# Retention into a maxout FFN: first weight loads moved ahead of a value load, the first two products cut into column parts, conversion steps put before copies

## The chip, the cores and the metric

The kernel runs on one core of a Trainium2 chip. The metric is device time in microseconds (us), measured around one execution; the profile's span runs from the first to the last instruction that the profiler recorded. All times below are us unless ns is written.

## The reference

Inputs: q, k, v of shape (8 batches, 8 heads, 576 positions, 64) in float32, and weights w1, w2, w3 (512 x 768) and w_out (768 x 512) in float64. What must come out:

```
scores = q k^T / sqrt(64)
D[i, j] = gamma_h ** (i - j)  for i >= j, else 0
attn    = (scores * D) v                       # per batch and head
x       = attn, put together to 4608 x 512     # token rows, heads side by side
h       = max(x w1, x w2, x w3)
out     = h w_out                              # 4608 x 512
```

## The kernel before, in words

The 4608 tokens are 36 **chunks** of C = 128 rows (a name with g is a chunk) and 9 **blocks** of 512 tokens, four chunks each (t is a block). A chunk's retention is a causal product within the chunk plus a carried state of 64 x 64 per head. For the first chunks the steps are functions called by hand, in the order in which their instructions go into the engines' queues:

- `load(g)` (L225): three transfers of 256 KB (k, q, v) on SP's queue; a chunk that crosses a batch's end has two halves each. The fourth chunk (CPT - 1 = 3) puts the load of one weight piece before its v, at L230.
- `transposes(g)` (L254): TensorE (PE) transposes k and q into PSUM, ScalarE (ACT) copies them out as kT and qT (L272).
- `scores(g)` (L274): 8 matmuls of qT and kT (L285), then VectorE (DVE) multiplies the two results by the causal mask into `st` (L201 is the recorded line of such steps).
- `decay(g)` (L241): GpSimd (POOL) scales v into `vd` (L249). `state(g)`: 8 matmuls `kv` (L352). `keep(g)`: DVE, and where a state goes on POOL too, makes the next state (L360 to L363).
- `values([g])` (L375): 8 matmuls of vd and st (L393), 8 of state and qT (L406), then `output` (L441): two DVE multiplications by `gq` into this chunk's columns of xT.

PE takes its queue in order, so a matmul that waits holds all that follow it. The same holds for DVE, ACT, POOL and SP.

Weights come as 24 **pieces** of 512 KB (18 of w1 to w3, each 128 columns wide, then 6 of w_out), each in two transfers of 256 KB (`load_weights`, L485). They are 64-bit floats, and `convert_all` (L614) turns them into fp32. Per pair of pieces there are the steps exponent (DVE L630, ACT L632), fraction (ACT L638, DVE L639, ACT L641), whole (DVE L644), sign (DVE L648) and product (DVE L656, which writes `w`); the first three pairs go piece by piece, and from the fifth on the exponent of the next pair is put before the sign and product of the one at hand (L692). `convert(n)` runs the next n steps of this list. Each finished piece asks for one more load. Six pieces are asked for at the start, and there is room for eight.

A transfer uses one of eight semaphores in turn (ACT's and SP's together), and an issue waits until the transfer eight places earlier has landed.

Block 0 is the stretch in which everything is still being loaded and converted. In `ffn(0)` (L791) nine units (fp, i) follow each other, each with two plain products `up_plain` (L779) of 128 x 512 outputs over a depth of 512, then `downs_plain`. The first product of all was already split: 384 columns, which need chunks 0 to 2, and 128 columns, which need chunk 3. After each product comes its `maximum`: an ACT copy (i = 0, L789) or a DVE maximum (L788). Between the units the steps for block 1's chunks 4 to 7 are woven in (`steps(1)`, L911): `scores(4)`, `state(4)` and `keep(4)` come right after the first unit. From block 1 on the work is a sparser product scheme (L760, L557) on converted weights.

The order before the first unit is written out from L867 on: loads of chunks 0 to 3 with the two small `gs` transfers on SP after chunk 1, one weight piece, chunk 4, four pieces; then chunk by chunk the steps above, all of chunk 3 done before the first product starts; `gq` is loaded by four ACT issues after the first transposes.

Of the kernel before, what the change touches and what calls it, by code (L numbers as in the profile page):

```python
# [45 lines left out]
ALU = mybir.AluOpType  # L46
PSUM = bass.MemoryType.PSUM

C = 128
NT = 4 * C  # L50
# [31 lines left out]
def kernel(  # L82
# [14 lines left out]
    nc = tc.nc  # L97
    P = 128
    B, H, S, D = q.shape
# [25 lines left out]

    gk = const.tile([C, H], FP32, name="gk")
    gs_of = const.tile([P, H], FP32, name="gs_of")
    gs = const.tile([P, NP], FP32, name="gs")  # L130
# [1 line left out]
    const.tile([P, FILL // 4], FP32, name="fill")  # L132
    gq = const.tile([P, NP, C], FP32, name="gq")
    nc.scalar.dma_start(gk[:], key_decay)
    nc.vector.memset(one[:], 1.0)
    nc.scalar.copy(first[:], one[:])

# [11 lines left out]
    def warm(n):  # L149

        ps = ps_y.tile([P, P], FP32, tag="y", name="warm")
        for _ in range(n):
            nc.tensor.matmul(ps[:], lhsT=ident[:], rhs=ident[:], start=True, stop=True)
# [15 lines left out]
    def spans(g):  # L169

        row = 0
        while row < C:
# [1 line left out]
            n = min(C - row, S - pos)  # L174
            yield row, b, pos, n
            row += n

    def half(j):
        return slice(D * j, D * (j + 1))

    def place(g, c):

# [39 lines left out]
                        t[r:r + 32, :, e, :],  # L222
                        src[b, :, pos:pos + 32, 32 * a:32 * a + 32].rearrange("h p i -> p h i"))

    def load(g):  # L225
        if g >= BY_PE and ("q", g) not in raws:
            load_blocks(g, *range(C // 32))
        for n, src in (("k", k), ("q", q), ("v", v)) if g < BY_PE else (("k", k), ("v", v)):
            if n == "v" and g == CPT - 1:
                load_weights(1)  # L230
            bufs = {"k": 3, "q": 2, "v": 4}[n]
            pool, bufs = (raw0, 1) if n != "v" and g < BY_PE and g % (bufs + 1) == bufs else (raw, bufs)
            if n == "v":
                t = vpool.tile([C, H, D], FP32, tag="v", name="vraw")
            else:
                t = pool.tile([C, H, D], FP32, tag=n, name=n + "raw", bufs=bufs)
            raws[n, g] = t
            for row, b, pos, m in spans(g):
                nc.sync.dma_start(t[row:row + m], src[b, :, pos:pos + m, :].rearrange("h p d -> p h d"))

    def decay(g):  # L241
        factor = gk[:].unsqueeze(2).to_broadcast([C, H, D])
# [6 lines left out]
        nc.gpsimd.tensor_tensor(vds[g][:], t[:], factor, op=ALU.mult)  # L249
# [479 lines left out]
    def convert(n):  # L729
        for _ in range(n):  # L730
            next(converting, None)
# [44 lines left out]
                    nc.sync.dma_start(out[t * NT + m * P:t * NT + (m + 1) * P, :], osb[:])  # L776
            yield

    def up_plain(t, h, fb, i):  # L779
        ps = (ps_x, ps_y)[fb % 2].tile([P, NT], FP32, tag="xy"[fb % 2], name="up")  # L780
        first_of_all = t == 0 and (fb, i) == (0, 0)
        for cols in (slice(0, NT - C), slice(NT - C, NT)) if first_of_all else (slice(0, NT),):
            for dc in range(NDC):
                nc.tensor.matmul(ps[:, cols], lhsT=w_sb[i, fb][:, dc * P:(dc + 1) * P], rhs=xT[t][:, dc, cols],  # L784
                                 start=dc == 0 and cols.start == 0, stop=dc == NDC - 1,
                                 skip_group_check=first_of_all)
        if i > 0:
            return lambda: nc.vector.tensor_tensor(h[:, fb, :], h[:, fb, :], ps[:], op=ALU.max)  # L788
        return lambda: nc.scalar.copy(h[:, fb, :], ps[:])  # L789

    def ffn(t):  # L791

        h = hpool.tile([P, NF, NT], FP32, tag="h", name="h")
        if t == 0:
            for fp, i in units:
                for fb in (2 * fp, 2 * fp + 1):
                    maximum = up_plain(t, h, fb, i)
                    if CPT not in qks:
                        maximum()
                        transposes(CPT)  # L800
                        convert(4)
                        continue
                    if (fp, i) == units[-1]:
                        maximum()
                        convert(2)
                        continue
                    convert(4 if (fp, i) in units[:2] else 2)
                    maximum()
                yield
            convert(3)  # L810
            for fb, _ in enumerate(downs_plain(t, h)):
                convert(2 if fb < 2 else 4 * len(pieces))
                if fb == 2:
                    while_converting.close()
                    late["pool"] = ctx.enter_context(tc.tile_pool(name="late", bufs=1))
                    late_room()
                    sums_of_outs()
                elif fb > 2:
                    chore({3: 4, 4: 0, 5: 2}[fb])
                if fb in (1, 3):  # L820
                    yield
            yield
            return
        if t == 1:
            spread.append(True)
            weight_sums(0)
            weight_sums(2)
        plain = 1 if t == 1 else None
        order = (1, 0, 2) if t == 1 else (0, 2, 1)
        total = sum(48 if fp == plain else 2 * len(PRODUCTS) for fp in order)  # L830
        count = parts = 0
        for fp in order:
            if fp != plain:
                while fp not in summed_fp:
                    chore()
            for step, cost in enumerate(up_plain_all(t, h, fp) if fp == plain else up(t, h, fp)):
                if fp == plain:
                    chore(4 if step == 4 else 8)
                elif step % 4 == 1 or step % 4 == 3 and len(urgent) > (2 if t == 1 else 6):
                    chore(len(urgent) > 0)  # L840
                elif step % 4 == 2 and chores and (t > 1 or NF // 2 - 1 not in summed_fp):
                    chores.popleft()()
                if step % 3 == 2:
                    scale()
                count += cost or 1
                if count * (NF // 2 * 3) >= (parts + 1) * total:
                    parts += 1
                    yield
            sums_of_hidden(h, fp)
            if fp == plain:  # L850
                weight_sums(fp)
        chore(len(urgent))
        for n, _ in enumerate(downs(t, h, order)):
            chore(4)
            scale(2)
            if n in (1, 3):
                yield
        yield

    def up_plain_all(t, h, fp):  # L860
        for fb in (2 * fp, 2 * fp + 1):
            for i in range(3):
                up_plain(t, h, fb, i)()
                yield 8


    warm(6)  # L867
    for g in range(CPT):
        load(g)
        if g == 1:  # L870
            for j in range(2):
                nc.sync.dma_start(gs[half(j)].unsqueeze(2), state_decay[half(j), :, D * j:D * j + 1])
    load_weights(1)
    load(CPT)
    load_weights(4)
    decay(0)
    transposes(0)
    for c in range(2):
        for b in range(2):
            nc.scalar.dma_start(gq[half(c), b::2, :], out_decay[half(b), NP // 2 * c:NP // 2 * (c + 1), :])  # L880
    warm(2)
    scores(0)
    transposes(1)
# [4 lines left out]
    scores(1)  # L888
    first_output()
    transposes(2)  # L890
    state_factors()
    decay(2)
    state(1)
    keep(1)
    values([1], [1])
    transposes(3)
    decay(3)
    scores(2)
    scores(3)
    state(2)  # L900
    keep(2)
    convert(2)
    values([2], [2])
    convert(2)
    values([3], [3])
    convert(4)
    keep(3)
    decay(CPT)
    convert(2)

    def steps(t):  # L911

# [97 lines left out]
```

## Time and profile before

| | us |
|---|---|
| median of 4 runs | 755.0 |
| lowest and highest of them | 754.3, 756.08 |
| profiled execution's own time | 754.3 |
| its span | 752.2 |
| PE busy | 744.3 (99% of the span) |
| DVE, ACT, POOL busy | 510.0, 319.8, 82.6 |
| granted TensorE clock | 1.000 |
| start of the first product of block 0 (PE L784) | 25.17 |
| start of the second unit of block 0 | 34.85 |
| start of block 0's down products (PE L771) | 99.76 |

PE is busy nearly all the time, so the page's averages say little about the change. Read the order of time instead: the timelines of the engines over the first 100 us, in which a bracket says how long the engine stood idle before a row and what ended that, and the list of what PE waited for. A row of a timeline gives start, length, engine, line, operation, output and inputs, and the count of instructions merged; PE rows count two passes for each matmul. A row's length includes the tail of its last instruction, so the next row of the same engine may start before it ends.

### The profile page before, as it was taken

The page shows a single profiled execution, that of the slowest core. Times are in us where ns is not written, and L with a number is a line of the kernel's source. Part 1 is how long each engine was busy: PE and PEld are TensorE (multiplying, and loading weights), DVE is VectorE, ACT ScalarE, POOL GpSimd, SP SyncE. Part 2 cuts the span into 40 slices and gives each one's busy share as a digit, 9 for nine tenths or more (in the row PEclk, how much of TensorE's full clock was granted, in tenths as well). Part 3 has the DMA queues.
Part 4 walks back from the last instruction along what each step waited for, and adds up shares of the span by engine and source line. Part 5 has one row for each costly group of instructions (what it writes and reads, how often), then busy time and mean ns, then how long its engine had stood idle before and what let it go on. Part 6 is the DMA issues. An engine that isn't in the chain of part 4 may idle for free.

```text
span 752.2 us, 16566 instructions
## 1 busy us (share of the span) xinstructions
PE 744.3 (99%) x6728; PEld 607.8 (81%) x6728; DVE 510.0 (68%) x856; ACT 319.8 (43%) x645; POOL 82.6 (11%) x103
## 2 busy tenths in 40 slices
PE   8899999999999999999999999999999999999998
PEld 7545545588888888888888888888888888888887
DVE  3998987857866765686567746675667656763662
ACT  3674531055245433544354335542454245414441
POOL 3110112002000100011010101010101010100000
PEclk9999999999999999999999999999999999999999
DMA  9996742505142514242343224232515141000001
GB/s 222 225 245 142 223 93 72 98 16 99 44 94 40 93 37 101 50 78 50 75 83 66 63 65 91 40 75 66 95 29 95 44 93 36 1 30 29 0 1 57
DMA packets 230204, 59.30 MB, mean 79 GB/s; under 512 B 210800, under 2 KB 228848, under 8 KB 230128
## 3 DMA queue, kind: packets, MB, share of 16 engines
q1 hardware_dynamic: 229264, 57.91, 35.6%
q8 instruction: 53, 0.87, 0.5%
q10 hardware_dynamic: 864, 0.33, 0.2%
q14 instruction: 23, 0.19, 0.1%
HBM read 48.76 MB, written 9.44 MB: 77 GB/s over the span
## 4 chain that ended last, share of the span: by engine, by line
PE 94%; DVE 3%; DMA 2%; SPq 1%; issue 0%; ACT 0%; ACTq 0%; DVEq 0%
PE a L760 19%; PE b L760 16%; PE dx L557 11%; PE up L784 8%; PE c L760 8%; PE dz L557 6%; PE e L760 5%; PE d L760 5%; PE sk L307 3%; PE down L771 3%; PE dy L557 3%; PE o L424 2%; PE o L431 2%; DMA bits<-in_moe_w_out_dram 1%; PE kv L310 1%; PE o L393 1%
## 5 line engine op out<-in xcount | busy, mean ns | idle before, releaser
L748 DVE TENSOR_TENSOR part<-part 128x512 f32<-128x512 f32 x161 | 111.3, 691 | 107.5 <-ACT part L745 105.2
L745 ACT COPY part<-b 128x512 f32<-128x512 f32 x115 | 67.4, 586 | 154.8 <-PE b L760 154.8
L748 DVE TENSOR_TENSOR h<-h,part 128x512 f32<-128x512 f32 x115 | 79.5, 691 | 29.1 <-ACT h L745 25.1
L784 PE MATMUL up<-xT,w 128*128 128x512 f32 (+2 forms) x200 | 85.0, 579 | 1.5 <-DVE w L656 1.5
L745 ACT COPY part<-a 128x512 f32<-128x512 f32 x92 | 53.9, 586 | 49.5 <-PE a L760 49.0
L784 PEld LDWEIGHTS up<-xT,w 128*128 128x128 f32 x200 | 36.7, 190 | 43.9 <-issue 39.9
L760 PE MATMUL a<-s,w 128*128 128x256 f32 x276 | 70.9, 379 | 0.0
L760 PE MATMUL b<-s,n 128*128 128x256 f32 x276 | 70.8, 379 | 0.0
L189 ACT ACTIVATE vraw<-vraw,gk 128x64 f32<-128x64 f32 x208 | 65.5, 347 | 1.0 <-DMA vraw<-in_v_dram 1.0
L760 PEld LDWEIGHTS b<-s,n 128*128 128x128 f32 x276 | 52.4, 190 | 7.1
L760 PEld LDWEIGHTS a<-s,w 128*128 128x128 f32 x276 | 52.4, 190 | 7.1
L527 POOL TENSOR_TENSOR H<-h 128x256 f32<-128x256 f32 x24 | 20.3, 844 | 310.1 <-DVE h L748 310.1
L760 PE MATMUL c<-xT,w 128*128 128x256 f32 x184 | 49.1, 389 | 0.0
L760 PE MATMUL b<-xT,n 128*128 128x256 f32 x184 | 47.2, 379 | 0.0
L760 PE MATMUL d<-s,w 128*128 128x256 f32 x184 | 47.2, 379 | 0.0
L324 POOL TENSOR_TENSOR s<-s,gs_of 64x512 f32<-64x512 f32 x21 | 22.5, 1070 | 211.1 <-DVE s L322 209.1
L557 PE MATMUL dx<-To,H 128*128 128x256 f32 (+1 forms) x204 | 44.9, 370 | 0.0
L760 PE MATMUL e<-xT,w 128*128 128x256 f32 x184 | 43.5, 379 | 0.0
L760 PE MATMUL a<-xT,n 128*128 128x256 f32 x184 | 43.5, 379 | 0.0
L557 PEld LDWEIGHTS dx<-To,H 128*128 128x128 f32 x204 | 36.6, 190 | 4.9
L760 PEld LDWEIGHTS e<-xT,w 128*128 128x128 f32 x184 | 35.0, 190 | 5.2 <-issue 0.2
L760 PEld LDWEIGHTS b<-xT,n 128*128 128x128 f32 x184 | 35.0, 190 | 4.8
(122 smaller groups left out, 1286.4 us busy)
## 6 DMA issues: line engine op xcount, KB each, us to landing
bits<-in_moe_w_dram SPq DMA_DIRECT2D x36, 256.0 KB, 5.5
out_dram<-osb SPq DMA_DIRECT2D x35, 256.0 KB, 2.1
kraw<-in_k_dram SPq DMA_DIRECT2D x32, 256.0 KB, 3.1
vraw<-in_v_dram SPq DMA_DIRECT2D x32, 256.0 KB, 3.7
qraw<-in_q_dram SPq DMA_DIRECT2D x224, 32.0 KB, 2.1
kxraw<-in_k_dram SPq DMA_DIRECT2D x224, 32.0 KB, 2.1
bits<-in_moe_w_out_dram SPq DMA_DIRECT2D x6, 512.0 KB, 5.8
qraw<-in_q_dram SPq DMA_DIRECT2D x6, 256.0 KB, 4.3
```

The lines of the kernel that those rows point to most:

```text
L189: scaling.popleft()()
L307: nc.tensor.matmul(s[half(c), h, :], lhsT=kT[half(c), h, :], rhs=qT[half(c), h, :], start=True, stop=True)
L324: nc.gpsimd.tensor_tensor(new, new, factor, op=ALU.mult)
L424: nc.tensor.matmul(o[m][half(c), n, u, :], lhsT=vds[g][half(m), h, :], rhs=sts[g][half(m), h, :], start=n == 0 and u == 0, stop=place(g, m ...
L431: nc.tensor.matmul(o[m][half(c), n, u, :], lhsT=stacks[g][half(m), h, :], rhs=qks[g]["q"][half(m), h, :], start=False, stop=True, skip_gro ...
L527: urgent.append(lambda: (pool(s3, a11, a21, op=ALU.subtract), pool(s4, a12, s2, op=ALU.subtract)))
L557: nc.tensor.matmul(o, lhsT=hS[n](fp)[:, m * P:(m + 1) * P], rhs=late["T"][n][:, fp, cols], start=first and fp == order[0] and (m == 0 or l ...
L745: nc.scalar.copy(of[step], ps[step[0]][:])
L748: nc.vector.tensor_tensor(of[dst], a, b, op=op)
L760: nc.tensor.matmul(ps[chain][:, e, :], lhsT=factor(w, 2 * fp + e), rhs=xS[t][x], start=n == 1 and e == 0, stop=ends, skip_group_check=True)
L771: nc.tensor.matmul(b[:], lhsT=h[:, fb, m * P:(m + 1) * P], rhs=w_sb["out", fb], start=(fb == 0), stop=(fb == NF - 1))
L784: nc.tensor.matmul(ps[:, cols], lhsT=w_sb[i, fb][:, dc * P:(dc + 1) * P], rhs=xT[t][:, dc, cols], start=dc == 0 and cols.start == 0, stop= ...
```

## The change

- `load_weights` and the loads of chunk 2 to 4 stand in another order on SP: the first weight piece comes before v of chunk 2, the second before v of chunk 3, the third and fourth before chunk 4, two more after it. `load` takes the names it is to load.
- The two `gs` transfers go from SP to the front of ACT's queue, and two of the four `gq` transfers move ahead of the first transposes' copies (`output_factors`).
- Chunk 2's scores, state and values now come before the transposes of chunk 3, and chunk 3's `decay` before them. Conversion steps come in between. `state_factors` (two small ACT copies) comes later.
- `up_plain` can cut its columns and gives back the remaining steps. `first_ups` puts the two first products out in two column parts each: 384 columns of the first, then chunk 3's state and values, then 384 columns of the second, then both products' last 128 columns, both ACT copies, and the `decay` and `transposes` of chunk 4. Conversion steps go in between. `scores(4)` follows at once.
- In the other units the conversion steps stand as before, except in the last one, where they now precede the first of the two maxima.

```diff
+    for j in range(2):
+        nc.scalar.dma_start(gs[half(j)].unsqueeze(2), state_decay[half(j), :, D * j:D * j + 1])
...
-    def up_plain(t, h, fb, i):
+    def up_plain(t, h, fb, i, *parts):
...
+        def products(a, b):
             for dc in range(NDC):
...
+        ends = [0, *parts, NT]
+        steps = [partial(products, a, b) for a, b in zip(ends, ends[1:])]
+        steps.pop(0)()
+        return (*steps, maximum)
+
+    def first_ups(h):
+
+        g = CPT - 1
+        rest0, copy0 = up_plain(0, h, 0, 0, g * C)
+        convert(2)
+        state(g)
+        convert(2)
+        values([g])
+        keep(g)
+        convert(2)
+        rest1, copy1 = up_plain(0, h, 1, 0, g * C)
+        convert(2)
+        for step in (rest0, copy0, rest1, copy1):
+            step()
+        decay(CPT)
+        transposes(CPT)
+        convert(4)
...
             for fp, i in units:
+                if (fp, i) == units[0]:
+                    first_ups(h)
+                    yield
+                    continue
                 for fb in (2 * fp, 2 * fp + 1):
-                    maximum = up_plain(t, h, fb, i)
...
-                    if (fp, i) == units[-1]:
+                    maximum, = up_plain(t, h, fb, i)
+                    if (fp, i) == units[-1] and fb % 2:
                         maximum()
                         convert(2)
-                        continue
-                    convert(4 if (fp, i) in units[:2] else 2)
-                    maximum()
+                    else:
+                        convert(4 if (fp, i) == units[1] else 2)
+                        maximum()
...
     warm(6)
-    for g in range(CPT):
-        load(g)
-        if g == 1:
-            for j in range(2):
-                nc.sync.dma_start(gs[half(j)].unsqueeze(2), state_decay[half(j), :, D * j:D * j + 1])
+    load(0)
+    load(1)
+    load(2, "kq")
     load_weights(1)
+    load(2, "v")
+    load(CPT - 1, "kq")
+    load_weights(1)
+    load(CPT - 1, "v")
+    load_weights(2)
     load(CPT)
-    load_weights(4)
+    load_weights(2)
     decay(0)
+    output_factors(0)
     transposes(0)
+    output_factors(1)
...
-    transposes(3)
-    decay(3)
     scores(2)
-    scores(3)
+    decay(CPT - 1)
+    convert(2)
     state(2)
     keep(2)
+    convert(1)
+    values([2], [2])
+    transposes(CPT - 1)
+    convert(1)
+    state_factors()
     convert(2)
-    values([2], [2])
-    convert(2)
-    values([3], [3])
-    convert(4)
-    keep(3)
-    decay(CPT)
-    convert(2)
+    scores(CPT - 1)
```

More of the change, by code (lines that the diff above doesn't have):

```diff
@@ L124, with half @@
     ctx.enter_context(tc.manual_schedule())
+    def half(j):
+        return slice(D * j, D * (j + 1))
     gk = const.tile([C, H], FP32, name="gk")
@@ L176, in spans @@
             row += n
-    def half(j):
-        return slice(D * j, D * (j + 1))
     def place(g, c):
@@ L223, in load_blocks, with load @@
                         src[b, :, pos:pos + 32, 32 * a:32 * a + 32].rearrange("h p i -> p h i"))
-    def load(g):
+    def load(g, names="kqv"):
         if g >= BY_PE and ("q", g) not in raws:
@@ L228, in load @@
         for n, src in (("k", k), ("q", q), ("v", v)) if g < BY_PE else (("k", k), ("v", v)):
-            if n == "v" and g == CPT - 1:
-                load_weights(1)
+            if n not in names:
+                continue
             bufs = {"k": 3, "q": 2, "v": 4}[n]
@@ L777, in downs_plain, with maximum @@
             yield
-    def up_plain(t, h, fb, i):
+    def up_plain(t, h, fb, i, *parts):
         ps = (ps_x, ps_y)[fb % 2].tile([P, NT], FP32, tag="xy"[fb % 2], name="up")
-        first_of_all = t == 0 and (fb, i) == (0, 0)
-        for cols in (slice(0, NT - C), slice(NT - C, NT)) if first_of_all else (slice(0, NT),):
+        def products(a, b):
             for dc in range(NDC):
[L784 to L789, printed above, removed]
+                nc.tensor.matmul(ps[:, a:b], lhsT=w_sb[i, fb][:, dc * P:(dc + 1) * P], rhs=xT[t][:, dc, a:b],
+                                 start=dc == 0 and a == 0, stop=dc == NDC - 1, skip_group_check=len(parts) > 0)
+        def maximum():
+            if i > 0:
+                nc.vector.tensor_tensor(h[:, fb, :], h[:, fb, :], ps[:], op=ALU.max)
+            else:
+                nc.scalar.copy(h[:, fb, :], ps[:])
+        ends = [0, *parts, NT]
[18 more added lines that the diff above has]
+        convert(4)
     def ffn(t):
@@ L795, in ffn @@
             for fp, i in units:
+                if (fp, i) == units[0]:
+                    first_ups(h)
+                    yield
+                    continue
                 for fb in (2 * fp, 2 * fp + 1):
-                    maximum = up_plain(t, h, fb, i)
-                    if CPT not in qks:
-                        maximum()
-                        transposes(CPT)
-                        convert(4)
-                        continue
-                    if (fp, i) == units[-1]:
+                    maximum, = up_plain(t, h, fb, i)
+                    if (fp, i) == units[-1] and fb % 2:
                         maximum()
                         convert(2)
-                        continue
-                    convert(4 if (fp, i) in units[:2] else 2)
-                    maximum()
+                    else:
+                        convert(4 if (fp, i) == units[1] else 2)
+                        maximum()
                 yield
@@ L862, in up_plain_all, with output_factors @@
             for i in range(3):
-                up_plain(t, h, fb, i)()
+                maximum, = up_plain(t, h, fb, i)
+                maximum()
                 yield 8
     warm(6)
-    for g in range(CPT):
-        load(g)
-        if g == 1:
-            for j in range(2):
-                nc.sync.dma_start(gs[half(j)].unsqueeze(2), state_decay[half(j), :, D * j:D * j + 1])
-    load_weights(1)
+    load(0)
+    load(1)
+    load(2, "kq")
+    load_weights(1)
+    load(2, "v")
[3 more added lines that the diff above has]
+    load_weights(2)
     load(CPT)
-    load_weights(4)
+    load_weights(2)
     decay(0)
-    transposes(0)
-    for c in range(2):
+    def output_factors(c):
         for b in range(2):
             nc.scalar.dma_start(gq[half(c), b::2, :], out_decay[half(b), NP // 2 * c:NP // 2 * (c + 1), :])
+    output_factors(0)
+    transposes(0)
+    output_factors(1)
     warm(2)
@@ L890 @@
     transposes(2)
-    state_factors()
     decay(2)
@@ L895 @@
     values([1], [1])
-    transposes(3)
-    decay(3)
     scores(2)
-    scores(3)
+    decay(CPT - 1)
+    convert(2)
     state(2)
     keep(2)
-    convert(2)
-    values([2], [2])
-    convert(2)
-    values([3], [3])
-    convert(4)
-    keep(3)
-    decay(CPT)
-    convert(2)
+    convert(1)
[3 more added lines that the diff above has]
+    state_factors()
+    convert(2)
+    scores(CPT - 1)
     def steps(t):
```

## The prediction, on record before the changed kernel ran

> **What bounds the kernel now.** I read the page's chain first, then the list of what PE waited for, then the engines' timelines over 100 us. Chain: PE holds 94% of the span, so a change pays only by what PE stops waiting for.
>
> ```profile
> span 752.2 us, 16566 instructions
> PE 94%; DVE 3%; DMA 2%; SPq 1%; issue 0%; ACT 0%; ACTq 0%; DVEq 0%
> ```
>
> PE's waits in the whole run (us in total, times, longest):
>
> ```profile
> PE up L784 <- DVE w L656: 1.5, 1, 1.5
> PE warm L153 <- POOL ident masks.py:199: 1.4, 1, 1.4
> PE s L285 <- ACT qT L272: 1.1, 2, 0.8
> PE o L393 <- POOL vd L249: 0.6, 1, 0.6
> PE down L771 <- DVE w_out L656: 0.3, 1, 0.3
> ```
>
> All that can be had is here: 1.5 before the first product, 1.1 and 0.6 in the chunks before it, 0.3 at the down products. In time, on PE:
>
> ```profile
> 12.63 0.60 PE L271 MATMUL qt<-ident,qraw 128*128 128x128 f32 x4
> 25.17 3.74 PE L784 MATMUL up<-xT,w 128*128 128x384 f32 x16 [1.47 <-DVE w L656]
> 42.70 7.03 PE L784 MATMUL up<-xT,w 128*128 128x512 f32 x16
> 49.66 1.16 PE L285 MATMUL s<-qT,kT 64*128 64x128 f32 x16
> 99.76 14.00 PE L771 MATMUL down<-w_out,h 128*128 128x512 f32 x32 [0.35 <-DVE w_out L656]
> ```
>
> and on ACT, POOL, DVE and SP:
>
> ```profile
> 9.92 0.59 ACT L272 COPY kT<-kt 128x512 f32<-128x512 f32 x1 [3.45 <-DMA gq<-in_out_decay_dram]
> 13.63 1.05 POOL L249 TENSOR_TENSOR vd<-vraw,gk 128x512 f32<-128x512 f32 x1 [3.31 <-DMA vraw<-in_v_dram]
> 20.45 1.04 POOL L249 TENSOR_TENSOR vd<-vraw,gk 128x512 f32<-128x512 f32 x1 [5.20 <-DMA vraw<-in_v_dram]
> 20.68 1.09 DVE L630 TENSOR_SCALAR expo<-bits 128x512 int32<-128x512 int32 x1
> 25.70 0.42 DVE L630 TENSOR_SCALAR expo<-bits 128x512 int32<-128x512 int32 x1
> ```
>
> The reader is to see three things: transfers set when vd and the weights are there (the windows show 230 to 260 GB/s from 5 to 20, 169 from 20 to 25, about 250 after), chunk 1's kT copy stood behind four gq issues, and a whole unit takes 6.96 (42.70 to 49.66).
>
> **The first stretch, to the second unit's start (34.85 before).** I walk PE's new order with start-to-start times from its timeline: a chunk's k and q transposes 0.9, scores 1.1, kv 0.55, o from st 1.0, o from state 0.6, a 512-column product 3.53 (29.62 to 33.15). Cut in 384 and 128 it took 3.58 (25.17 to 28.75), so the second cut costs 0.05; I take 2.65 and 0.9 for the parts.
>
> - *ACT's queue.* Two gs issues (0.88 and 0.62 on SP) stand before the table load, two gq issues (0.66 each in its timeline) before the first kT copy: 0.83 + 0.44 + 1.5 + 1.28 + 0.19 + 1.3 = 5.55 against 5.26, so s(0) starts about 0.3 later, at 6.8. Only two gq issues now precede chunk 1's kT: it comes at about 9.0 instead of 9.92, and s(1) at 10.4 instead of 11.04, right behind o(0). The waits of 0.85 and 0.2 are gone. What is late next: q of chunk 2, which landed at 12.33; the bytes ahead of it are nearly the same. So qt of chunk 2 starts at 12.35 instead of 12.63 and the gain kept is 0.3. Its price is unknown in one point: gs now shares the wires with the first k and q. Bounds: nothing, or 1.0 (what gs and gq took between the landings of v1 at 9.21 and k2 at 11.31, less one transfer). I take nothing: the 0.6 of slack at s(1) covers most of it.
> - *Weights ahead of v2.* o from state of chunk 1 ends at 15.4 (before 15.73), s(2) at 16.5. v2 landed 1.23 after q2. Now two weight transfers come first; these landed 1.39 and 1.24 apart (17.37, 18.61 after q3's 15.98). v2 lands at 12.3 + 1.3 + 1.2 + 1.2 = 16.0, vd ends 1.1 later, kv(2) at 17.1: a **new wait of 0.6**. Bounds: no wait, if v2 is there by 15.4 (one transfer per 1.03, as k3 to q3); 1.2, if it takes the 1.77 that v3 took behind weights. Behind that matmul stand all others.
> - *Chunk 3.* kv, o, o to 19.25, transposes to 20.15. Now scores(3) follows its own transposes. Chunk 2's row prices that: qt started at 12.63, its copy ended at 13.96, so scores can start 1.35 after qt, and PE has work for 0.45 of it. **New wait of 0.9**; s(3) 21.05 to 22.15. Before, s(2) lay between.
> - *First product.* w of piece 0: both transfers are there by 14.8; DVE does exponent and fraction after st of chunk 2 (17.4), whole, then xT of chunk 2 (to 20.0), sign and product, 0.6 each: 21.3, ahead of 22.15. The 1.47 wait is gone, with 0.85 in hand.
> - *The rest.* 2.65 to 24.8; chunk 3's kv, o, o 2.15 to 26.95 (vd3: v3 lands by about 22.2, where before the same set of bytes was in; slack over 1); 2.65 to 29.6; the last columns 1.8 to 31.4; chunk 4's transposes to 32.3, and scores(4) follows at once, with both h copies ahead of kT on ACT: again **0.9**; before, the second product lay between. s(4) 33.2, kv(4) 34.3, second unit at **34.85**: no gain, 1.5 + 1.1 + 0.6 removed, 0.6 + 0.9 + 0.9 and the delay at the start put in, and the later order of chunk 3 uses up the remainder. Bounds from v2 and gs: 34.2 to 35.8.
>
> *A lock.* DVE's exponent took 1.09 beside POOL's vd at 20.45 and 0.42 without. w of piece 1 is due at 26.95; I have st of chunk 3 to 23.5, then three steps of 0.6, 25.4; a POOL step may add up to its 1.04, 26.4. The Trainium skill, "SBUF — State Buffer", section "SBUF: two separate sides", goes further: VectorE and GpSimd hold their shared port pair exclusively for a whole instruction and the loser blocks, when VectorE has two SBUF inputs or a two-port mode. By that page each step that newly lies beside a POOL step could be blocked in turn, and if three were, the sum would be 1 longer; by the row it stays as it is.
>
> **The second stretch, 34.85 to 99.76.** Where PE ran freely, units took 6.96. The fourth started at 50.75 and the fifth at 57.90: 7.15, because w was written at 57.84; 0.2 lost. The last ran from 92.28, down started at 99.76: 7.48, 0.5 lost to w_out. In the last unit exponent, sign and product of w_out (0.60 + 1.26 + 1.23) stood behind a maximum that PE released at 96.02; now they start after st at 94.0 and end near 97.2, ahead of 99.3; their bits were read by ACT at 89.97. For the fifth unit DVE must write w by 57.7: exponent, fraction and whole of piece 0 now lie before 20.4, when DVE was in part idle, and exponent and fraction no longer take the 1.92 beside POOL that they took at 20.68 and 21.70; I count 1 to 2 of lead, less waits for s(3) and o(3) of about 0.7. It suffices: **-0.7**. If that cover is gone, the 0.2 stays.
>
> After 99.76 PE waits for nothing and the order is the same. **Sum:** 0.0 - 0.7. The profiled run of 754.3 (span 752.2 and 2.1 around it) becomes 753.6. It was the lowest of the runs, 0.7 below their median; the median of 755.0 becomes **754.3**.
>
> **Rivals.**
>
> - *No wait for v2, the small waits shorter.* v2 by 15.4 removes 0.6, and qT may be a little quicker: second unit at 34.0 to 34.2, sum -1.5 to -1.8, about 753.3. For it: k3 followed by q3 within 1.03. Against: v3 behind weights took 1.77.
> - *DVE or gs keep what is won* (the change does not do what it says): w of piece 0 after 22.15, or w at 57.84 as before, or first k later. Sum between -0.4 and +0.7, about 755.0.
> - *Slower: the weights of unit four.* DVE has the exponent of pair 5 (L630 at 47.36) in front of sign and product of pair 4; its bits landed at 46.98, and w came 3.5 after that, at 50.46, for a unit at 50.75. The same bytes come first in either order; but if the stream pauses once more as it did in 20 to 25 (169 GB/s, some 1.5 lost), they land at 48.5 or later. From 47.3 on each us is one of PE. With two such pauses +1.7 to +2.5, about 757.0. Against: chunk 4's six half transfers now follow four weight transfers of 1.1 each, so more is in flight.
>
> **Numbers.** About 0.2%, 1.5, is what a measurement tells from no change. Forecast 0.55 (753.6 to 755.0); first rival 0.20, about faster by over 0.2%; second 0.14, within; third 0.11, slower. So faster 0.20, same 0.69, slower 0.11. The range takes the first rival's and the bounds of v2 and gs: 752.8 to 755.9.
>
> **What would show it.** Right: no wait of the first product for w, it starts near 22; PE waits of 0.9 before s of chunks 3 and 4 for qT, some 0.6 at kv of chunk 2 for vd; second unit within 0.7 of 34.85; no wait of down. Wrong: the second unit before 34 or after 35.8, a wait for w at units four or five, any difference after the down products.

## The result, and the profile after

The changed kernel takes 753.91 us (median of 33 runs, 753.47 to 755.05); the kernel before, over all its runs beside it, 754.8 (53 runs). The ratio is 0.9987, with a 95% interval of 0.9982 to 0.9992: a gain of 0.9 that the interval separates from none, though it is less than the 0.2% (1.5) that the forecast took as the least that a measurement tells from no change. Forecast were 754.3, from 755.0, and a range of 752.8 to 755.9. The profiled execution took 753.61, its span 751.2.

Time and span do not fall by the same amount. Between the two profiled executions the span falls by 1.0 and the time by 0.7; the median span over all recorded runs falls by 1.2 (752.8 to 751.6), the median time by 0.9. What lies outside the span is 2.0 to 2.2 in every recorded run of the kernel before and 2.3 to 2.4 in every one of the changed kernel. Of the experiments below, e1, e7 and e8 have 1.9 to 2.2 and all others 2.3 to 2.5. No trace reaches outside the span, so the cause stays open; where two kernels differ in this, their spans are compared too.

The profile page of the changed kernel, its span and the shares of the chain that ended last by engine:

```profile
span 751.2 us, 16577 instructions
PE 99%; ACT 0%; DVE 0%; issue 0%; POOL 0%; POOLq 0%
```

Before, PE held 94% of that chain and DVE and transfers the rest; now it is PE nearly alone. The list of what PE waited for (us in total, times, longest), changed kernel:

```profile
PE s L287 <- ACT qT L274: 1.7, 3, 0.8
PE warm L158 <- POOL ident masks.py:199: 1.4, 1, 1.4
PE kv L354 <- POOL vd L251: 0.4, 1, 0.4
PE o L395 <- DVE xT L203: 0.2, 1, 0.2
```

The first product's wait for w (1.5), the one for vd of chunk 3 (0.6) and that of the down products for w_out (0.3) are off the list. In their place, scores wait for qT three times instead of two, and kv for vd. Where these waits stand is in PE's timeline (changed kernel):

```profile
10.41 1.16 PE L287 MATMUL s<-qT,kT 64*128 64x128 f32 x16
...
12.00 0.60 PE L273 MATMUL qt<-ident,qraw 128*128 128x128 f32 x4
...
16.63 0.69 PE L354 MATMUL kv<-vd,kraw 128*64 128x64 f32 x16 [0.36 <-POOL vd L251]
...
20.87 1.16 PE L287 MATMUL s<-qT,kT 64*128 64x128 f32 x16 [0.73 <-ACT qT L274]
21.96 2.85 PE L786 MATMUL up<-xT,w 128*128 128x384 f32 x8
...
26.82 4.63 PE L786 MATMUL up<-xT,w 128*128 128x384 f32 x24
...
33.11 1.16 PE L287 MATMUL s<-qT,kT 64*128 64x128 f32 x16 [0.78 <-ACT qT L274]
...
34.81 7.13 PE L786 MATMUL up<-xT,w 128*128 128x512 f32 x16
...
50.71 14.00 PE L786 MATMUL up<-xT,w 128*128 128x512 f32 x32
...
91.96 7.13 PE L786 MATMUL up<-xT,w 128*128 128x512 f32 x16
98.93 13.90 PE L773 MATMUL down<-w_out,h 128*128 128x512 f32 x32
```

The kernel before, two rows of the same timeline, and the row of unit five in the list of its chain:

```profile
34.85 7.13 PE L784 MATMUL up<-xT,w 128*128 128x512 f32 x16
...
92.28 7.13 PE L784 MATMUL up<-xT,w 128*128 128x512 f32 x16
```

```profile
57.90 7.13 PE up L784 x16
```

The first product starts 3.2 earlier (21.96, before 25.17), and yet the second unit starts where it did: 34.81, before 34.85. Units four and five now run as one row (50.71, 14.00), without a gap between them; before, unit five came 7.15 after unit four instead of 6.96. Down starts 6.97 after the last unit's start (91.96) instead of 7.48, and at 98.93 instead of 99.76. So in these two executions the front gave 0.04 and the second stretch 0.79 up to the start of the down products.

Why the down products waited is on DVE. Before, the maximum that PE released at 96.02 stood ahead of the last steps of w_out, whose product ended at 99.71:

```profile
96.02 0.69 DVE L788 TENSOR_TENSOR h<-h,up 128x512 f32<-128x512 f32 x1 [2.04 <-PE up L784]
...
98.48 1.23 DVE L656 TENSOR_TENSOR w_out<-mant,expo 128x1024 f32<-128x1024 f32 x1
```

In the changed kernel that product ended at 96.68, 2.25 ahead of its use:

```profile
95.45 1.23 DVE L658 TENSOR_TENSOR w_out<-mant,expo 128x1024 f32<-128x1024 f32 x1
```

### The profile page after: what moved, and what is told of

It reads as the page before. It is cut to its first block, busy times and chain, and to the rows that moved or that the text cites. A ratio compares the mean times of both kernels' runs of the same rounds, so it can differ in the third digit from the quotient of the medians.

```text
span 751.2 us, 16577 instructions
## 1 busy us (share of the span) xinstructions
PE 744.6 (99%) x6736; PEld 608.9 (81%) x6736; DVE 511.1 (68%) x856; ACT 320.2 (43%) x645; POOL 84.0 (11%) x103
## 3 DMA queue, kind: packets, MB, share of 16 engines
q1 hardware_dynamic: 228720, 57.91, 35.8%
## 4 chain that ended last, share of the span: by engine, by line
PE 99%; ACT 0%; DVE 0%; issue 0%; POOL 0%; POOLq 0%
PE a L762 19%; PE b L762 16%; PE dx L559 11%; PE up L786 11%; PE c L762 8%; PE dz L559 6%; PE e L762 5%; PE d L762 5%; PE sk L309 3%; PE down L773 3%; PE dy L559 3%; PE o L426 2%; PE o L433 2%; PE s L287 1%; PE o L395 1%; PE kv L312 1%
## 5 line engine op out<-in xcount | busy, mean ns | idle before, releaser
L762 PEld LDWEIGHTS a<-xT,n 128*128 128x128 f32 x184 | 35.0, 190 | 4.8
```

The costliest lines, as they stand in the source:

```text
L762: nc.tensor.matmul(ps[chain][:, e, :], lhsT=factor(w, 2 * fp + e), rhs=xS[t][x], start=n == 1 and e == 0, stop=ends, skip_group_check=True)
```

## The experiments

Theory A is the forecast's: the moved loads, conversions and cut products trade old waits of PE for new ones and come out even; the gain is two waits that leave the second stretch. Theory B: it is the lead which the new front gives DVE that brings the gain. Each experiment gives its median and, because such a median is uncertain by some tenths, the profile beside it.

### The last unit's order alone (e1) and without it (e2)

Put into the kernel before (e1), and its condition taken out of the changed kernel (e2):

```diff
-                    if (fp, i) == units[-1]:
+                    if (fp, i) == units[-1] and fb % 2:
                         maximum()
                         convert(2)
                         continue
```

> The kernel before, with one edit of the change alone: in the last unit of block 0 the conversion steps stand before the first of the two maxima. Theory A (the gain of the change is two waits that leave the second stretch, 0.5 to 0.6 at the down products by this edit and 0.2 at unit five by the front): the first product stays at 25.17, the second unit at 34.85, unit five still starts late (7.15 after unit four); down starts 0.4 to 0.5 earlier and loses its wait of 0.35; time 0.5 to 0.6 below before. Theory B (w_out comes sooner because the new front gives DVE a lead): this edit without the front does less than 0.2.

> The changed kernel without that one edit: in the last unit the maximum comes first again. Theory A: the wait of down for w_out is back (0.35 in the list of waits, down 7.4 to 7.5 after the last unit's start instead of 6.97), time 0.5 to 0.6 above the changed kernel, 0.3 below before. Theory B: down starts where it does in the changed kernel, no difference from it.

Measured: e1 753.98 (ratio to before 0.9992, 0.9983 to 1.0001), e2 755.3 (1.0009, 1.0001 to 1.0018); before beside them 754.73. One line in the old kernel brings 0.75 in time and 0.9 in span (752.7 to 751.8), most of the 0.9 and 1.2 that the whole change brings; the interval of e1 alone just reaches no change, so its timeline has to show what the line does. Without it the changed kernel is 0.6 slower than the kernel before (0.3 in span), and 1.4 slower than the changed kernel, where 0.5 to 0.6 was expected. PE's timeline of e1:

```profile
34.38 7.13 PE L784 MATMUL up<-xT,w 128*128 128x512 f32 x16
...
50.28 14.17 PE L784 MATMUL up<-xT,w 128*128 128x512 f32 x32
...
91.70 7.13 PE L784 MATMUL up<-xT,w 128*128 128x512 f32 x16
98.67 13.90 PE L771 MATMUL down<-w_out,h 128*128 128x512 f32 x32
```

Down follows the last unit by 6.97 without a wait, while unit five still loses 0.17 (14.17 against 14.00 for two free units). In e2, PE, then DVE and POOL at the same place:

```profile
92.86 7.13 PE L786 MATMUL up<-xT,w 128*128 128x512 f32 x16
101.08 14.00 PE L773 MATMUL down<-w_out,h 128*128 128x512 f32 x32 [1.08 <-DVE w_out L658]
```

```profile
96.60 0.69 DVE L791 TENSOR_TENSOR h<-h,up 128x512 f32<-128x512 f32 x1 [2.05 <-PE up L786]
97.21 0.69 DVE L632 TENSOR_SCALAR expo<-bits 128x1024 int32<-128x1024 int32 x1
97.81 1.23 DVE L650 SCALAR_TENSOR_TENSOR expo<-bits,expo 128x1024 int32<-128x1024 int32 x1
99.08 1.95 DVE L658 TENSOR_TENSOR w_out<-mant,expo 128x1024 f32<-128x1024 f32 x1
```

```profile
98.83 1.11 POOL L251 TENSOR_TENSOR vraw<-vraw,gk 128x512 f32<-128x512 f32 x1 [12.96 <-DMA vraw<-in_v_dram]
```

DVE stood idle for 2.05 until PE released the maximum, with w_out's three steps behind it, and here the last of them met a POOL step and took 1.95 instead of 1.22. Down came 8.22 after the unit's start, not the 7.4 to 7.5 expected: theory A had the wait, not the POOL step. Theory B is out for the down products: the front's lead does nothing as long as the maximum stands in front.

### Transposes of chunks 3 and 4 moved off their scores (e3), of chunk 4 alone (e5)

e3 has both parts of this diff, e5 only the second:

```diff
     convert(1)
-    values([2], [2])
     transposes(CPT - 1)
+    values([2], [2])
     convert(1)
...
         convert(2)
-        for step in (rest0, copy0, rest1, copy1):
-            step()
         decay(CPT)
         transposes(CPT)
+        for step in (rest0, copy0, rest1, copy1):
+            step()
         convert(4)
```

> The changed kernel with the transposes of chunk 3 put ahead of chunk 2's values, and those of chunk 4 ahead of the last 128 columns of the first two products, so that PE has work between transposes and scores. Theory A (the two waits of 0.73 and 0.78 before scores are the price of the new order, and behind them the weight stream sets unit five): both waits go, the second unit starts at 33.3 to 33.6 instead of 34.81, but DVE still writes w of unit five at about 57.3, since it waits for bits that land at 45.9; so unit five starts at about 57.4 instead of 57.67 and the time is 0.3 below the changed kernel. Rival C (DVE and the stream move forward with PE): the whole 1.3 to 1.5 arrives, 752.4 to 752.6. Rival D (w of the first product becomes the wait, since it is written at 21.2): second unit at 34 or later, no gain.

> The changed kernel with chunk 4's transposes alone put ahead of the last 128 columns of the first two products (chunk 3's stay where the change has them). Theory A: the wait of 0.78 before scores of chunk 4 goes; from the start of chunk 3's scores to the second unit it is 13.2 instead of 13.94. But DVE writes w of unit five 11.4 after its neighbour's bits land (45.9 to 57.3 in the changed kernel), with 0.34 in hand, so unit five follows unit four by 7.3 to 7.4 instead of 6.96, and the time is 0.3 below the changed kernel, about 753.6. Rival C (DVE has enough in hand): no wait at unit five, 0.8 below, 753.1. Rival E (as when both were moved: another operand becomes the wait in the first stretch): no gain or a loss.

e3: 754.61 (1.0002, 0.9992 to 1.0011), from 752.78 to 756.9, a wider spread than any other kernel; the profiled execution is the slowest of them. PE and DVE there:

```profile
18.76 0.63 PE L273 MATMUL qt<-ident,qraw 128*128 128x128 f32 x4 [0.80 <-DMA qraw<-in_q_dram]
...
24.40 4.51 PE L786 MATMUL up<-xT,w 128*128 128x384 f32 x8 [2.30 <-DVE w L658]
```

```profile
21.04 0.76 DVE L203 TENSOR_TENSOR xT<-o,gq 128x256 f32<-128x256 f32 x2 [1.36 <-PE o L408]
21.71 1.52 DVE L650 SCALAR_TENSOR_TENSOR expo<-bits,expo 128x512 int32<-128x512 int32 x1
23.27 0.98 DVE L658 TENSOR_TENSOR w<-mant,expo 128x512 f32<-128x512 f32 x1
```

Both waits for qT are gone, as expected, and rival D's wait is there. q of chunk 3 landed at 18.62, so the transposes themselves waited; chunk 2's values, now behind them, came later, and on DVE xT stands ahead of sign and product of piece 0, which then ran beside POOL's vd. w was written at 24.25, 2.3 after PE wanted it. Less would be lost in an execution where q lands earlier; the lowest time, 752.78, fits that, but there is no second profile that shows it.

e5: 752.89 (0.9971, 0.9961 to 0.9981), 1.0 below the changed kernel. Its PE timeline:

```profile
30.51 1.95 PE L786 MATMUL up<-xT,w 128*128 128x128 f32 x16
32.39 1.16 PE L287 MATMUL s<-qT,kT 64*128 64x128 f32 x16
33.48 0.68 PE L354 MATMUL kv<-vd,kraw 64*64 64x64 f32 x16
34.09 7.13 PE L786 MATMUL up<-xT,w 128*128 128x512 f32 x16
...
49.99 14.00 PE L786 MATMUL up<-xT,w 128*128 128x512 f32 x32
```

No wait before chunk 4's scores, 13.1 from chunk 3's scores (20.99) to the second unit instead of 13.94, and none at unit five: w was written at 55.31 for a use at 56.95. The cap that I expected at unit five did not hold here (rival C); the last runs come back to that.

### Chunk 3 by another way (e9), and both once more side by side (e11, e12)

e9 and e12 add to e5 a split of chunk 2's values, and let DVE write w of piece 0 first:

```diff
+        if between:
+            between()
         for m, g in enumerate(chunks):
             old = before(g)
...
-    convert(1)
-    values([2], [2])
-    transposes(CPT - 1)
-    convert(1)
+    convert(2)
+    values([2], [2], between=partial(transposes, CPT - 1))
     state_factors()
```

> The kernel with chunk 4's transposes moved (752.89), and the same idea at chunk 3: its transposes stand between the two halves of chunk 2's values (o from st, transposes, o from state), and on DVE sign and product of piece 0 go ahead of chunk 2's xT, which moving the whole had put in front of them. Theory A (each wait of scores for qT is a price of the order, and no operand is behind it once DVE's order follows): the wait of 0.73 before chunk 3's scores falls to 0.1 to 0.2, the first product starts at 21.5 to 21.7 instead of 22.09, time 0.4 to 0.6 lower: 752.4. Rival (q of chunk 3 lands at 17.3 to 18.6 and the o from state stands behind its transposes, or w of piece 0 is beside POOL's vd): the wait moves to the transposes or to the first product, no gain or a loss.

> The kernel with chunk 4's transposes moved, beside the next one on the same chip. Theory A (the whole wait before chunk 4's scores is gain): 752.9 again, second unit at 34.1 to 34.4, 718.7 from there to the end.

> The kernel with chunk 3's transposes between the halves of chunk 2's values as well. In its first profile it took 6.43 from chunk 2's scores to the first product where the kernel beside it took 6.86. Theory A: those 0.4 reach the end, 752.5. Rival (what PE saves there it waits for elsewhere, at a later operand or at the first transfers): no difference, 752.9.

e9: 752.82 (0.9976, 0.9967 to 0.9985), no difference from e5. Side by side: e11, which is e5's kernel, 753.2 (0.9982, 0.9973 to 0.9991); e12, e9's kernel, 752.74 (0.997, 0.9961 to 0.9979). From chunk 2's scores to the first product the two take 6.85 (15.29 to 22.14) and 6.43 (15.47 to 21.90); of e12:

```profile
20.81 1.16 PE L287 MATMUL s<-qT,kT 64*128 64x128 f32 x16 [0.31 <-ACT qT L274]
21.90 2.85 PE L788 MATMUL up<-xT,w 128*128 128x384 f32 x8
```

The wait fell from 0.73 to 0.31 and the 0.42 saved agrees with the 0.46 between the medians; with intervals of 0.7 each way that is consistent, not proved, and e9 beside e5 had not shown it. Against the kernel before beside them, e9 and e12 are 2.1 faster, e5 2.1 and e11 1.6. In e11's profile the cap at unit five is there after all:

```profile
57.97 2.41 PE L786 MATMUL up<-xT,w 128*128 128x512 f32 x5 [0.78 <-DVE w L658]
```

Unit five follows unit four by 7.92 (50.05 to 57.97), 0.96 too late: the bits landed at 46.66, DVE had waited 1.44 for them, and POOL's vd held its last step up by 0.73. In e12's profile unit five is late too (7.63 after unit four). So theory A and rival C are both true, each in some executions, by when the weights land and where POOL's step falls.

### The exponent behind the product (e6)

```diff
-            if following:
+            if following and n != 4:
                 following.exponent(both)
             two.sign(both)
             yield
             two.product(both)
+            if following and n == 4:
+                following.exponent(both)
             yield
```

> The kernel of the run above, with the exponent of the fifth pair of pieces on DVE put behind the product of the fourth instead of ahead of its sign, so that DVE does not stand before bits that land at 45.9 (0.88 idle in the changed kernel). Theory A: that wait of DVE goes, w of unit four comes 1.3 to 1.5 earlier and w of unit five up to 0.9 earlier; unit five then waits for nothing, and the 0.78 of the run above reaches the end: 753.1. Rival: the fraction of that pair on ACT now starts later and w of unit five is as late as before; no difference from the run above.

753.04 (0.9975, 0.9966 to 0.9984), against e5's 752.89: nothing gained. In its profile w of unit five is written at 57.24, 0.18 after it was due (6.96 after unit four's 50.10), in e5's at 55.31, ahead of it; POOL's vd held its product for 1.94 instead of 1.22, and the bits had landed later in the execution, so the two profiles do not tell whether the edit helps DVE. It stays open; there is no sign that it does.

### v of chunk 2 first (e4), gs and gq where they were (e8)

```diff
-    load(2, "kq")
-    load_weights(1)
-    load(2, "v")
+    load(2)
+    load_weights(1)
```

> The changed kernel with v of chunk 2 loaded ahead of the first weight piece again. Theory A: the wait of 0.36 before kv of chunk 2 goes, and the 0.16 before o of chunk 1 may stay; the weights of piece 0 land about 1 later (15.5) and are still in time for DVE at 17.5; first product 0.3 to 0.4 earlier, second unit at 34.4 to 34.5; of that 0.3 reaches the end: 753.6. Rival: the first weights now come too late for DVE, w of piece 0 after 22, the first product waits as it did before, second unit later than 34.81.

> The changed kernel with gs back on SP after chunk 1 and all four gq issues behind the first copy of kT on ACT, as before. Theory A (the move saves the wait of 0.85 before chunk 1's scores, and costs little at the first k and q): the wait is back, 0.7 to 0.9; q of chunk 2 sets what is kept, so the second unit starts 0.2 to 0.5 later, and since unit five has 0.34 in hand the time is 0.2 to 0.5 above the changed kernel. Rival (gs between the first transfers delays chunk 1's k by 0.5, and q of chunk 2 rules anyhow): no difference or a gain.

e4: 753.96 (0.9993, 0.9984 to 1.0001); e8, which puts the two gs transfers back behind chunk 1 on SP and all gq issues behind the first kT copy: 754.06 (0.999, 0.9981 to 0.9999). In time neither differs from the changed kernel; in span e4 does not either (751.5), but e8 does (752.1, the changed kernel 751.6). In e4 kv of chunk 2 waits no more, but two waits of 0.16 for st stand right behind it: from chunk 2's scores to chunk 3's transposes it takes 3.95 (15.61 to 19.56), in the changed kernel 3.94 (15.11 to 19.05). The wait for vd had covered that for st, so nothing was to be had. In e8 the wait before chunk 1's scores is back:

```profile
11.32 1.16 PE L285 MATMUL s<-qT,kT 64*128 64x128 f32 x16 [0.88 <-ACT qT L272]
```

Part of it is had back at the start: in this profile q of chunk 0 landed at 4.70, in the changed kernel at 4.98, and chunk 0's scores start at 6.46 instead of 6.81. The rest stays: q of chunk 2 landed at 12.27, well before its transposes (12.91), so it does not rule what follows, and e8's median span is 0.5 longer. Inside the span the move of gs and gq is thus worth 0.5, the upper end of theory A. In time only 0.15 of it is seen, as e8 spends 0.3 less outside the span; that e7, which has the move, is as short there speaks against the move as the reason.

### Weights of unit four later (e7)

Two more transfers of 256 KB are put ahead of that pair:

```diff
-            at(0, (load, b))
+            def again(g):
+                for e in range(2):
+                    nc.sync.dma_start(w_out[:, 2, e, :].rearrange("p (h d) -> p h d", d=D),
+                                      k[e, :, 0:C, :].rearrange("h p d -> p h d"))
+
+            at(0, (load, b), (again, b))
```

> The changed kernel with two more transfers of 256 KB (k rows copied to a place that nobody reads at that time) behind chunk 5's load, ahead of the weights of unit four's pair. The slower rival of the forecast: the bits land 2.1 to 2.3 later, the exponent that stands in front of unit four's sign and product starts at about 48.2 instead of 46.03, unit four's w comes 0.4 after it is wanted, and unit five's w 1.8 after: time 1.7 to 2.1 above the changed kernel, 755.7 to 756.0. Rival (DVE makes it up in the idle time that it has): within 0.5 of the changed kernel.

754.73 (0.9995, 0.9986 to 1.0004), 0.8 above the changed kernel (1.1 in span, 752.7): between the two expectations. DVE and PE there:

```profile
47.67 0.71 DVE L632 TENSOR_SCALAR expo<-bits 128x1024 int32<-128x1024 int32 x1 [1.09 <-issue]
...
57.05 1.23 DVE L658 TENSOR_TENSOR w<-mant,expo 128x1024 f32<-128x1024 f32 x1
```

```profile
50.97 7.13 PE L786 MATMUL up<-xT,w 128*128 128x512 f32 x16
58.33 7.13 PE L786 MATMUL up<-xT,w 128*128 128x512 f32 x16 [0.23 <-DVE w L658]
```

The exponent started at 47.67, unit four did not wait, and unit five came 7.36 after it, 0.40 too late. DVE needs 10.6 from that exponent to w of unit five (58.28), which is due at 57.93, so in this execution the wait starts when the exponent is later than 47.3. The forecast named 47.3 for unit four, which did not wait here; that the two numbers agree is chance. Nor is the 10.6 fixed: in e11, where POOL's vd held a step up, DVE needed 11.1 (46.78 to 57.91), and 46.78 was too late. My expectation of 1.8 at unit five was too high in three terms: the exponent came at 47.67 and not at 48.2, DVE needed 10.6 from it and not the 11.3 of the changed kernel's first profile (46.03 to 57.33, with POOL's vd in the way), and unit four itself started 0.26 later.

### The changed kernel again (e10)

> The changed kernel itself, for a second profile of it and times beside the run above. If its first profiled execution was typical, the second unit starts at 34.8 and w of unit five is written 0.3 ahead of its use. If the other runs with this front are the typical ones (second unit at 35.1 to 35.7, w of unit five 1.9 to 2.2 ahead), it was an early one, and the front as it stands costs about 0.5 at the second unit and gives 0.2 back at unit five. Time 753.9 either way.

753.94 (0.9992, 0.9983 to 1.0001). PE's timeline of this execution (754.21):

```profile
17.64 0.69 PE L354 MATMUL kv<-vd,kraw 128*64 128x64 f32 x16 [0.79 <-POOL vd L251]
...
35.49 7.13 PE L786 MATMUL up<-xT,w 128*128 128x512 f32 x16
```

The second unit starts 0.68 later than in the first profile, and the rows show it in transfers: v of chunk 2 landed at 16.47, there at 15.46, and k and q of chunk 1 0.3 and 0.7 later. From the second unit on, the two executions agree within 0.1. That holds for others too; span minus the second unit's start (from the unrounded spans):

| kernel | own time | span | second unit | from there to the end of the span |
|---|---|---|---|---|
| before | 754.30 | 752.2 | 34.85 | 717.3 |
| e1, before with the last unit's order | 753.05 | 751.0 | 34.38 | 716.6 |
| changed | 753.61 | 751.2 | 34.81 | 716.4 |
| e10, changed again | 754.21 | 751.9 | 35.49 | 716.4 |
| e2, changed without that order | 755.77 | 753.4 | 35.72 | 717.7 |
| e3, both transposes moved | 756.90 | 754.5 | 38.07 | 716.4 |
| e4, v of chunk 2 first | 754.02 | 751.7 | 35.32 | 716.4 |
| e7, weights of unit four later | 754.14 | 752.0 | 35.07 | 716.9 |
| e8, gs and gq back | 754.12 | 752.1 | 35.73 | 716.4 |
| e5 | 752.80 | 750.5 | 34.09 | 716.4 |
| e6, e5 with the exponent behind | 753.34 | 750.9 | 34.20 | 716.7 |
| e9 | 752.82 | 750.5 | 34.08 | 716.4 |
| e11, e5 again | 754.02 | 751.6 | 34.15 | 717.5 |
| e12, e9 again | 753.40 | 751.1 | 33.91 | 717.1 |

The last column is 716.4 wherever neither the down products nor unit five wait. Every row above that has such a wait in its timeline: 0.2 in e1 (unit five), 0.9 before (0.3 around unit five, 0.6 at the down products), 1.3 in e2 (down), and 0.3 to 1.1 in e6, e7, e12 and e11 (unit five). So the column settles both waits, the one at down and the one at unit five. Own times do not show it as clearly, because of the 0.3 that lies outside the span in some kernels and not in others. Taking the column as fixed, the median spans put the second unit of a middling execution at 752.8 - 717.3 = 35.5 before and at 751.6 - 716.4 = 35.2 in the changed kernel: an estimate, by which the front gains about 0.3 and the second stretch 0.9, and 0.3 of that is lost outside the span.

## Why the prediction was right, step by step

- **ACT's queue.** Foretold: scores of chunk 0 at 6.8, of chunk 1 at 10.4, nothing for gs. Measured: 6.81, 10.41. The 6.8 was met by luck. The first kT copy did not come at 5.55 but at 5.25, as before (5.26): the two gq issues (2.68 to 3.98) ran beside the table load (2.62 to 3.90), where the sum has one after the other. The scores were late because the qT copy came at 6.17 (before 5.88), after q transposes that took 1.10 instead of 0.83; q of chunk 0 had landed at 4.98 instead of 4.80. The wait of 0.85 is gone; that of 0.2, which the forecast had as gone too, is still there (0.23 before chunk 0's scores). q of chunk 2 came earlier than I had it (11.48 for 12.33, transposes at 12.00 for 12.35); in the second profile 12.72. e8 puts the whole move of gs and gq at a gain of 0.5 in span, where the forecast kept 0.3.
- **Weights ahead of v2.** A wait of 0.6, between none and 1.2. Measured: 0.36 in the changed kernel, 0.79 and 1.12 in two other executions of the same front (e10, e2), 0.19 in e11, none in e5, e6 and e7, where v landed at 14.83, 14.96 and 14.29. The size is the transfer's, not the code's.
- **Chunks 3 and 4.** 0.9 at each scores; measured 0.73 (0.72 in e8) and 0.78 in every profile in which the transposes stand there. Scores start 1.33 and 1.38 after q's transposes, as the row had it (1.35); these keep PE for 0.60 of it, not 0.45. The experiments show that these were real prices: chunk 4's taken off brings 0.7 (e11) to 1.0 (e5); for chunk 3's, e12 is 0.46 below e11, while e9 is no lower than e5. A forecast that had seen only the waits that go (1.5 + 1.1 + 0.6) would have missed them.
- **First product.** Foretold at 22.15 with w at 21.3; measured 21.96 and 21.23. The parts took 2.78 and 4.47 together 7.25, where the old two products took 3.58 and 3.53: the second cut costs 0.14, not 0.05.
- **Second unit.** 34.85 foretold, 34.81 measured; but the closeness is partly luck, as e10's 35.49 says. The waits of PE from chunk 0's scores to the second unit fall from 3.08 (0.85, 0.16, 0.60, 1.47) to 2.03 (0.16, 0.36, 0.73, 0.78), that is by 1.05, and 0.04 of it arrives. The forecast left such a remainder to the later order of chunk 3. What takes up most of it is small steps: chunk 0's scores start 0.29 later; o from st of chunk 2 takes 1.30 (17.15 to 18.45) instead of 1.0, because the second half of its st is only written at 17.59 (where vd came later, in e10 and e2, it took 0.98 and 0.97); the q transposes ahead of the two new waits take 0.60 each, some 0.1 more; the second cut takes 0.14.
- **Second stretch.** -0.7 foretold, of which 0.2 at unit five and 0.5 at down. Measured between the two profiles 0.19 and 0.51, and in both places a further 0.1 inside the products that had waited (unit five to the o behind it 7.06 before and 6.97 after, down 14.00 and 13.90), which I had not counted: 0.9. The forecast's 753.6 for the profiled execution, measured 753.61, is therefore two errors that cancel: the span fell by 1.0 and not by 0.7, and the 2.1 around it, taken as fixed, became 2.4. No run shows why. e1 and e2 show the larger part directly. For unit five the reason was DVE's lead: w was written 0.33 ahead of its use in the changed kernel and 2.2 in e2; it was 0.13 late before and 0.02 late in e1.
- **The rivals.** "DVE or gs keep what is won" did not happen. The slower one did not happen by itself; e7 made something like it happen, with the wait at unit five and not at unit four.

What the forecast left out: the cover at the last unit is thinner than the row said. Without the new order the wait for w_out is 0.5 (before) or 1.25 (e2), by whether POOL's step falls on DVE's last one; in these two profiles that is why the edit is worth 0.75 in one kernel and 1.4 in the other.

## What to carry to other kernels

Count the waits that an edit puts in as carefully as those that it takes out: an operation put directly behind its own producer waits for the copy between them (0.73 and 0.78 here); with 1.88 of independent work between, the wait was gone (e5), with 0.6 it was still 0.31 (e12). When a change of many parts moves the time a little, try its smallest part alone; here one condition carried most of it. And before explaining a tenth of a microsecond between two profiles, subtract the stretch that transfers decide and what lies outside the span: the same kernel's second unit moved by 0.68 between two executions, and the time outside the span differs by 0.3 between two kernels.

## What the runs showed of the hardware

In these rows a DVE step that works in SBUF and meets a POOL step does not slow down, it stands still until POOL is done. In e2 the product L658 started at 99.08 beside POOL's step of 98.83 to 99.94 and ended at 101.03, that is POOL's end and its own 1.22 less 0.13. In the changed kernel the sign L650 started at 29.62 beside POOL's 29.21 to 30.60 and ended at 31.15: 30.60 and 0.68 less 0.13. The forecast's own row comes out the same way: the exponent that took 1.09 at 20.68 ended at 21.77, and POOL's 21.49 and 0.42 less 0.13 is 21.78. The other way round POOL's step of 1.04 took 1.39 at 29.21, behind DVE's L646 (29.02 to 29.70). The mask multiplication, which reads PSUM, took 1.27 at 22.68 beside POOL's 22.43 to 23.22, no longer than its 1.29 alone. This is what the Trainium skill, "SBUF — State Buffer", section "SBUF: two separate sides", says of the port pair that the two engines share: whoever starts first holds it for the whole instruction. Here the runs agree with it. What the forecast allowed, one POOL step at most, was enough for w of piece 1 (25.87, between its 25.4 and 26.4). The lock did not decide this change, since DVE had time in hand, but it sets by how much a late weight is late (e2, e11).
